# Seven products for every block of layer one, the sign in the evictions, and finer waits

## The chip, the cores and the metric

The kernel runs on one core of a Trainium2 chip. The metric is the time of one execution in microseconds (us); 607.39 us is the median of the three runs before the change. Engines are named as the profile names them: PE is TensorE's matmul, PEld its weight load, DVE VectorE, ACT ScalarE, POOL GpSimd, SP SyncE, which here only issues transfers.

## The reference

Attention over 2 batches, 8 heads, 768 positions and a head width of 64, with a causal window of `n_local` = 96 positions, `n_global` = 8 positions that all see, and a bias by distance; then two layers of a feed-forward network on the 1536 tokens:

```python
x = attn_out.transpose(0, 2, 1, 3).reshape(B * S, H * D)      # 1536 x 512
g = s * np.maximum(x @ moe_w_in, 0) ** 2 + b                  # 512 -> 2048
x = g @ moe_w_out                                             # 2048 -> 512
g = np.maximum(x @ moe2_w_in, 0) ** 2
return g @ moe2_w_out
```

The input `s` is drawn positive, but the kernel takes either sign: it works with |s| and keeps the sign in a column `sg`.

## The kernel before

Each float32 operand is split into a rounded part `hi` and a rest `lo`, and a product is three matmuls (hi·hi, hi·lo, lo·hi). The splits are one copy (ACT or POOL) and one subtraction (DVE). Weights come as 64-bit words; four steps (`d0` on ACT, `d1` to `d3` on DVE, L41 to L56) turn 512 KB of them into a 128x512 tile.

**Stages.** The attention takes twelve tiles of 128 tokens, from the start to about 127 us. From 24.7 us its matmuls are interleaved on PE with the first four of layer one's sixteen weight chunks (`h`, `y`). The other twelve chunks of layer one, and then all sixteen of layer two, are taken in pairs (`a`, `a`+1) and two token halves (`tp`) of 768 tokens, and a pair with one half is a block. Two pairs form a group; a group's order is pair, pair on half 0, then pair, pair on half 1. The groups of layer one are pairs 4 and 6, 8 and 10, 12 and 14.

**A block's first weight.** The 256 x 512 weights and 512 x 768 tokens are cut in 2 x 2. A plain block (`plain`, L541) makes four products of 12 matmuls of 384 columns. A seven-product block (`product`, L530) makes seven products of 6 such matmuls, from four weight sums S1 to S4 (`wsum`, DVE) and four column sums of the input, T1 to T4. Three products accumulate in place; the others are put together by five DVE instructions from PSUM and a copy `m1` (`mid`, `cadd`, L552 to L572). Then come relu and square (ACT), `gh` (ACT or POOL), `gl` (DVE), and the second weight's matmuls (`y2`, L624). `PLAIN` (L31) lists the plain blocks: pairs 4 and 6 on both halves, four of the twelve; all of layer two is seven-product.

**Column sums.** For layer one they come from the attention's hi and lo parts (`tsum1`, L506, task `zs`): eight for each half, one for each T and row tile, in the order T3, T1, T2, T4, in a single buffer `tq`. Each is split by `zsh` and `zsl`. T1 is written over the input's second block, so its split waits for the plain products of its half (`d1`). For layer two the sums (`tsum`, L498, task `ts`) come from `acc`, in the single buffer `m1` that the blocks' copy `m1` uses too. The first product of a block of layer two waits for all eight splits and three input splits of its half, that of a seven-product block of layer one for all eight splits:

```python
                add(("p",) + u + (s,), {"PE": 1.047}, lambda e, u=u, s=s: f.product(*u, s),
                    [prev] + [("wsl", x, a) for x in need[s]] + extra[s] + dt * (s == 0), tm + 1.05 * s,
```

**Evictions.** At a group's end six `flush2` instructions on DVE add the PSUM banks to `acc`. After layer one's last group, four ACT passes for each half multiply `acc` by `sg` (task `sg`, L665 to L667); then the parts are split (`xh`, `xl`) and summed (`ts`).

**Order.** `order` (L805) lists all tasks with engines, estimated times, dependencies, a due time and the rings that they occupy, and `Plan.run` (L135) walks through them at build time: an engine that is free takes the ready task with the earliest due time. That order is the program's; on the chip each engine takes its instructions strictly in it. `SHIFT` (L69) moves single due times.

Of the kernel before, what the change touches and what calls it, by code (L numbers as in the profile page):

```python
# [118 lines left out]


class Plan:
# [1232 lines left out]
```

## Time and profile before

| | |
|---|---|
| runs before | 607.23, 607.39, 608.9 us; median 607.39 |
| profiled execution | 606.85 us |
| its span, first to last instruction | 605.1 us |
| busy: PE, DVE, ACT, POOL | 591.4, 496.8, 354.5, 113.7 us |

The profiled execution's own time is 1.7 us more than its span, which leaves out what lies around the program, and 0.54 us less than the median of the runs. A duration on PE is longer than the distance from one matmul to the next, since matmuls overlap: the start times tell what one costs.

### The profile page before, as it was taken

To read this page: it belongs to the slowest core of one execution; us is meant where nothing else is said; L and a number is where in the kernel's file an instruction comes from. 1 tells how busy PE (TensorE), PEld (TensorE's weight loads), DVE (VectorE), ACT (ScalarE), POOL (GpSimd) and SP (SyncE) were. 2 spreads that over 40 slices of the span, in tenths; PEclk is the share of its full clock that TensorE was granted. 3 is DMA by queue.
4 is the path that set the end of the run, shared out by engine and by line. 5 is a ranking of instruction groups with operands and counts; after the bars stand their busy time and mean duration, and the time that the engine had idled before them with its cause. 6 is when DMAs were issued, how large, how long until landed. Compare 5 with 4: busy or idle time off the path is not lost.

```text
span 605.1 us, 10174 instructions
## 1 busy us (share of the span) xinstructions
PE 591.4 (98%) x3705; PEld 533.9 (88%) x3705; DVE 496.8 (82%) x1115; ACT 354.5 (59%) x774; POOL 113.7 (19%) x187
## 2 busy tenths in 40 slices
PE   8999999999999999999999899999999999999995
PEld 5788898999999999999999788899899999899984
DVE  7999898877999799987989999989587978774452
ACT  7999897756754445544667585655354645434330
POOL 5464432101112111111201012213010111000000
PEclk9999999999999999999999999999999999999999
DMA  7775641022321200312130302241222122000023
GB/s 283 286 268 182 218 157 39 3 96 73 111 70 36 80 26 1 110 61 74 51 124 1 104 2 70 69 140 35 70 69 90 51 69 71 35 1 1 0 106 109
DMA packets 14889, 52.11 MB, mean 86 GB/s; under 512 B 1904, under 2 KB 2160, under 8 KB 14832
## 3 DMA queue, kind: packets, MB, share of 16 engines
q1 hardware_dynamic: 14832, 51.39, 25.2%
q8 instruction: 31, 0.51, 0.3%
q14 instruction: 26, 0.21, 0.1%
HBM read 48.24 MB, written 3.15 MB: 85 GB/s over the span
## 4 chain that ended last, share of the span: by engine, by line


## 5 line engine op out<-in xcount | busy, mean ns | idle before, releaser
L538 PE MATMUL h<-xh,u 128*128 128x384 f32 x384 | 111.7, 337 | 1.2 <-ACT m L221 1.2
L641 PE MATMUL yy<-u,gh 128*128 128x512 f32 x360 | 111.8, 392 | 0.0
L635 PE MATMUL yy<-gh,u 128*128 128x512 f32 (+1 forms) x384 | 97.7, 337 | 0.2 <-ACT gh L605 0.2
L538 PE MATMUL h<-th,u 128*128 128x384 f32 x288 | 85.6, 338 | 0.0
L641 PEld LDWEIGHTS yy<-u,gh 128*128 128x128 f32 x360 | 67.2, 188 | 11.8
L635 PEld LDWEIGHTS yy<-gh,u 128*128 128x128 f32 x384 | 66.8, 189 | 8.5 <-ACT gh L605 0.5
L225 POOL TENSOR_SCALAR u<-st 128x512 fp32r<-128x512 f32 (+1 forms) x47 | 35.2, 749 | 202.4 <-PE h L538 58.7
L538 PEld LDWEIGHTS h<-xh,u 128*128 128x128 f32 x384 | 70.5, 188 | 2.6 <-ACT m L221 1.5
L641 PE MATMUL yy<-u,gl 128*128 128x512 f32 x180 | 70.4, 391 | 0.7 <-DVE gl L615 0.7
L635 PE MATMUL yy<-gl,u 128*128 128x512 f32 (+1 forms) x192 | 64.9, 338 | 1.8 <-DVE gl L612 1.8
L538 PE MATMUL h<-xl,u 128*128 128x384 f32 x192 | 64.6, 337 | 0.0
L538 PEld LDWEIGHTS h<-th,u 128*128 128x128 f32 x288 | 53.1, 188 | 1.9 <-DVE u L559 0.4
L221 ACT ACTIVATE u<-st 128x512 fp32r<-128x512 f32 (+1 forms) x41 | 26.2, 639 | 44.6 <-PE h L538 13.4
L221 ACT ACTIVATE st<-st 128x512 f32<-128x512 f32 x64 | 42.8, 676 | 11.7 <-DMA st<-in_moe_w_in_dram 8.0
L52 DVE SCALAR_TENSOR_TENSOR st<-st 128x512 int32<-128x512 int32 x64 | 46.1, 723 | 3.7 <-ACT st L221 0.9
L538 PE MATMUL h<-tl,u 128*128 128x384 f32 x144 | 48.5, 337 | 0.0
L375 ACT ACTIVATE sn<-sn,nm 128x256 f32<-128x256 f32 (+1 forms) x96 | 46.0, 483 | 1.4 <-DVE nm L367 1.3
L55 DVE SCALAR_TENSOR_TENSOR st<-st 128x512 int32<-128x512 int32 x64 | 44.8, 700 | 0.9
L594 ACT ACTIVATE r<-r 128x384 f32<-128x384 f32 x64 | 33.6, 526 | 13.6 <-DVE r L589 9.0
L635 PEld LDWEIGHTS yy<-gl,u 128*128 128x128 f32 x192 | 36.3, 189 | 5.9 <-DVE gl L612 2.1
L641 PEld LDWEIGHTS yy<-u,gl 128*128 128x128 f32 x180 | 33.8, 188 | 8.5 <-DVE gl L615 1.1
L585 ACT ACTIVATE u<-u 128x384 f32<-128x384 f32 x32 | 16.7, 522 | 37.6 <-DVE u L572 37.5
(153 smaller groups left out, 1308.9 us busy)
## 6 DMA issues: line engine op xcount, KB each, us to landing
st<-in_moe_w_in_dram SPq DMA_DIRECT2D x32, 512.0 KB, 3.9
st<-in_moe_w_out_dram SPq DMA_DIRECT2D x32, 512.0 KB, 3.6
q<-in_qk_dram SPq DMA_DIRECT2D x10, 768.0 KB, 5.0
v<-in_v_dram SPq DMA_DIRECT2D x10, 512.0 KB, 4.6
out_dram<-acc SPq DMA_DIRECT2D x11, 256.0 KB, 2.3
q<-in_qk_dram SPq DMA_DIRECT2D x2, 512.0 KB, 5.0
v<-in_v_dram SPq DMA_DIRECT2D x2, 256.0 KB, 6.0
out_dram<-acc SPq DMA_DIRECT2D x2, 128.0 KB, 3.1
```

Source lines behind the costliest of these rows:

```text
L52: nc.vector.scalar_tensor_tensor(out=lo, in0=hi, scalar=3, in1=lo, op0=ALU.logical_shift_left, op1=ALU.bitwise_or)
L55: nc.vector.scalar_tensor_tensor(out=lo, in0=hi, scalar=-(1 << 31), in1=lo, op0=ALU.bitwise_and, op1=ALU.bitwise_or)
L221: nc.scalar.activation(out=out, in_=in_, func=AF.Copy, scale=scale)
L225: nc.gpsimd.tensor_scalar(out=out, in0=in_, scalar1=scale, scalar2=0.0, op0=ALU.mult, op1=ALU.add)
L375: self.nc.scalar.activation(out=sn[:, x], in_=sn[:, x], func=AF.Exp, scale=-1.0, bias=self.nm[:, n, h:h + 1], accum_out=self.rs[:, n, h:h ...
L538: self.nc.tensor.matmul(ps, p, q, start=first and kt == 0 and x == 0, stop=kt == 1 and x == 2, skip_group_check=not first)
L585: nc.scalar.activation(out=r, in_=h, func=AF.Relu, scale=rt)
L594: nc.scalar.activation(out=r, in_=r, func=AF.Square)
L635: self.nc.tensor.matmul(yj, p[:, js], q[:, lo:hi], start=first and x == 0 and not (side and j % 2), stop=last and x == 2 and not (side and ...
L641: self.nc.tensor.matmul(y[m], p[:, ms], q, start=first and x == 0, stop=last and x == 2)
```

## The change

- `PLAIN` is empty: pairs 4 and 6 of layer one are seven-product blocks like the others.
- The sign `sg` is multiplied in by the evictions (a three-operand instruction on DVE, a scaled copy for the first), and the four `sg` passes for each half are gone.
- Each of a block's seven products waits for the column sum or input part that it reads, and for no other.
- The sums of layer two use the buffer `tq` and wait only for the flushes of the rows that they read.
- The input test is three tasks (a maximum, a transpose on PE, the rest), placed ahead of block (26, 0) of layer two. It was one task after the attention.
- Another `SHIFT` table, a table `PIN` that fixes the engine of some 140 tasks, a time `TURN` that the plan charges when PE changes its kind of matmul, and small corrections of estimated times.

```diff
-PLAIN = ((4, 0), (6, 0), (4, 1), (6, 1))
+PLAIN = ()
...
+TURN = ((0.0, 0.09, 0.18, 0.08), (0.095, 0.0, 0.095, 0.095), (0.095, 0.095, 0.0, 0.095), (-0.08, 0.09, 0.09, 0.0))
+KIND = {"qk": 1, "pv": 2, "tr": 3}
...
+                    if e == "PE":
+                        k = KIND.get(self.tasks[t][0][0], 0)
+                        free[e] += TURN[kind][k]
+                        kind = k
...
-            self.T["t", tp, kt] = self.tm.tile([P, SB], F32, tag="m1", name=f"t{step}_{tp}_{kt}")
+            self.T["t", tp, kt] = self.tq.tile([P, SB], F32, tag="tq", name=f"t{step}_{tp}_{kt}")
...
-                nc.vector.tensor_tensor(out=a, in0=y, in1=a, op=ALU.add)
-            elif part == 1:
-                a = accT[:, j, t0:t0 + TB]
-                copy_r(nc, e, a, a, self.sg)
+                nc.vector.scalar_tensor_tensor(out=a, in0=y, scalar=self.sg, in1=a, op0=ALU.mult, op1=ALU.add)
...
-            self.nc.vector.tensor_tensor(out=a, in0=y, in1=a, op=ALU.add)
-        else:
-            copy_r(self.nc, e, a, y)
+            self.nc.vector.scalar_tensor_tensor(out=a, in0=y, scalar=self.sg, in1=a, op0=ALU.mult, op1=ALU.add)
+        else:
+            copy_r(self.nc, e, a, y, self.sg)
...
+        if name in PIN:
+            engs = {e: d for e, d in engs.items() if e.replace("DVX", "DVE") == PIN[name]}
...
+        if u == (26, 0):
+            add(("check", 0), "DVE:0.35", lambda e: f.check(0), ["second"], tc - 20)
+            add(("check", 1), {"PE": 0.15}, lambda e: f.check(1), [("check", 0), prev], tm, acq=[("h", "chk")])
+            add(("check", 2), "DVE:1.3", lambda e: f.check(2), [("check", 1)], tc, rel=[("h", "chk")])
+            prev = ("check", 1)
...
+        tl = lambda x: [("zsl" if one else "tsl", tp, kt, x) for kt in range(2)]
+        xl = lambda j: ["second"] if one else [("xl", "x", tp, j)]
+        dt = (xl(0), tl(1), xl(2), tl(3), tl(0), tl(2), xl(3))
...
-                    [prev] + [("wsl", x, a) for x in need[s]] + extra[s] + dt * (s == 0), tm + 1.05 * s,
+                    [prev] + [("wsl", x, a) for x in need[s]] + extra[s] + dt[s], tm + 1.05 * s,
...
-            for j in range(4):
-                add(("sg", tp, j), "ACT:0.85", lambda e, g=g, tp=tp, j=j: f.flush2(g, tp, j, 1, e),
-                    [last[j], last[4 + j // 2]], k)
...
-                    [("sg", tp, j // 2 * 2), ("sg", tp, j // 2 * 2 + 1)], k)
+                    [last[2 * r], last[2 * r + 1]] + [last[4 + r]] * c, k)
...
-                        sgn(kt) + [("tsl",) + v + (x - 1,)] * (x > 0) + [("tsl", tp, 0, 3)] * (kt > 0), k,
-                        acq=[("m1", "t") + v + (x,)] * new)
+                        [[last[kt], last[4]], [last[kt + 2], last[5]], [], []][x] + [("tsl",) + v + (x - 1,)] * (x > 0) +
+                        [("tsl", tp, 0, 3)] * (kt > 0), k,
+                        acq=[("tq", "t") + v + (x,)] * new)
```

`dt` is in the order of the seven products: the first needs the input's first part, the second T2, then a part, T3, T1, T4 and a part.

## Rows read from the trace of the kernel before

**Rows 1.** Page, part 1: busy us (share of the span) xinstructions.
```profile
PE 591.4 (98%) x3705; PEld 533.9 (88%) x3705; DVE 496.8 (82%) x1115; ACT 354.5 (59%) x774; POOL 113.7 (19%) x187
```
**Rows 2.** Windows: from:to length, busy us (count) of PE PEld DVE ACT POOL, clock, DMA.
```profile
0.00:24.70 24.70, 21.64 (x167) 14.26 (x168) 19.47 (x103) 20.17 (x71) 12.32 (x37) 1.00 0.86 336
...
100.00:127.60 27.60, 27.60 (x277) 25.48 (x277) 20.55 (x67) 19.45 (x56) 5.09 (x10) 1.00 0.01 1
127.60:145.20 17.60, 17.52 (x147) 17.34 (x147) 15.52 (x37) 10.18 (x20) 2.40 (x4) 1.00 0.25 91
145.20:213.90 68.70, 68.70 (x411) 64.96 (x409) 60.61 (x108) 38.40 (x68) 9.54 (x13) 1.00 0.27 85
213.90:334.50 120.60, 120.60 (x692) 112.28 (x691) 108.36 (x200) 69.65 (x123) 17.06 (x22) 1.00 0.17 53
334.50:391.00 56.50, 52.62 (x270) 46.42 (x269) 54.94 (x101) 38.06 (x69) 9.85 (x14) 1.00 0.22 65
```
**Rows 3.** Timeline of PE, borders of 36 plain and 36 seven-product matmuls: start, duration us.
```profile
192.97 0.34 PE L549 MATMUL h<-xh,u 128*128 128x384 f32 x1
...
199.21 0.40 PE L635 MATMUL yy<-gh,u 128*128 128x512 f32 x1
...
213.90 0.34 PE L538 MATMUL h<-xh,u 128*128 128x384 f32 x1
...
220.18 0.39 PE L635 MATMUL yy<-gh,u 128*128 128x512 f32 x1
```
**Rows 4.** Waits of PE: waiter <- releaser: us in total, times, longest.
```profile
PE yy L635 <- DVE gl L612: 1.8, 1, 1.8
...
PE h L538 <- ACT m L221: 1.2, 1, 1.2
...
PE yy L641 <- DVE gl L615: 0.7, 1, 0.7
```
**Rows 5.** Groups by form: line engine op out<-in xcount | busy us, mean ns | idle before.
```profile
L475 DVE TENSOR_TENSOR u<-st,u 128x512 fp32r<-128x512 f32 x36 | 25.9, 732 | 4.1 <-PE yy L641 3.2 <-PE yy L635 0.9
...
L572 DVE TENSOR_TENSOR u<-h,u 128x384 f32<-128x384 f32 x48 | 26.5, 553 | 13.1 <-PE h L538 12.8
...
L612 DVE SCALAR_TENSOR_TENSOR gl<-r,sgb,gh 128x384 fp32r<-128x384 f32 x32 | 19.5, 609 | 4.6 <-POOL gh L609 3.7 <-ACT gh L605 0.8
L615 DVE TENSOR_TENSOR gl<-r,gh 128x384 fp32r<-128x384 f32 x32 | 17.9, 559 | 4.1 <-ACT gh L607 2.4 <-POOL gh L609 1.7
...
L458 DVE TENSOR_TENSOR st<-st,st 128x256 f32<-128x256 f32 x36 | 16.4, 478 | 0.3
```
**Rows 6.** Instructions of the plain weight split: ns shortest/median/longest, first and last start us.
```profile
L441 DVE TENSOR_TENSOR u<-st,u x40: 660/684/889, 15.0 to 536.0; 128x512 fp32r<-128x512 f32 x40
```
**Rows 7.** Timeline at two of the turn's waits: start, duration us, engine, instruction [idle before].
```profile
372.45 0.55 DVE L615 TENSOR_TENSOR gl<-u,gh 128x384 fp32r<-128x384 f32 x1
372.92 0.55 DVE L504 TENSOR_TENSOR t<-acc 128x384 f32<-128x384 f32 x1
...
380.44 0.56 DVE L523 TENSOR_TENSOR tl<-t,th 128x384 fp32r<-128x384 f32 x1 [0.59 <-ACT th L221]
...
381.75 0.50 ACT L221 ACTIVATE m<-h 128x384 f32<-128x384 f32 x1
...
382.30 0.44 PE L538 MATMUL h<-xh,u 128*128 128x384 f32 x1 [1.15 <-ACT m L221]
```
**Rows 8.** Windows, tile tq alone (DVE ACT POOL): layer one's column sums with splits.
```profile
127.60:237.00 109.40, 32.05 (x56) 5.77 (x11) 3.72 (x5) 1.00 0.21 68
```
**Rows 9.** Windows, line 774 alone: the first chunks' y after the first plain product.
```profile
145.20:164.00 18.80, 6.23 (x50) 5.98 (x48) 1.00 0.40 124
```
**Rows 10.** Windows, all engines: a stretch inside layer one with DVE nearly full.
```profile
175.00:200.00 25.00, 25.00 (x148) 23.82 (x147) 24.59 (x45) 12.88 (x23) 4.20 (x6) 1.00 0.07 22
```
**Rows 11.** Windows, tile chk alone: the input test (PE, PEld, DVE).
```profile
140.00:145.00 5.00, 0.27 (x1) 0.08 (x1) 1.35 (x10) 1.00 0.01 2
```
**Rows 12.** Windows, all engines: from the last matmul to the end of the span.
```profile
598.40:605.10 6.70, 0.05 (x1) 0.00 (x0) 0.75 (x2) 0.00 (x0) 0.00 (x0) 0.87 0.26 88
```

More of the change, by code (lines that the diff above doesn't have):

```diff
@@ new lines @@
+SHIFT = {('at', 2, 0): 33.9, ('at', 3, 3): -39, ('at', 6, 3): 19.8, ('at', 7, 1): 22.2, ('at', 7, 3): -16.6, ('at',
+    9, 2): 47, ('cadd', 10, 1, 1, 0): -83.9, ('cadd', 14, 1, 1, 0): 138, ('cadd', 16, 0, 0, 1): -56, ('cadd', 18, 0,
+    0, 1): 32.3, ('cadd', 24, 0, 1, 1): -68.8, ('cadd', 28, 0, 1, 1): -48.5, ('cadd', 4, 0, 0, 1): -48.7, ('cadd',
[21 rows of a table added]
+    1): -12.5, ('norm', 4, 1): 170.3, ('norm', 4, 2): 40.3, ('norm', 5, 0): -22.9, ('norm', 6, 1): -2.8, ('norm', 7,
[7 rows of a table added]
+    ('qk', 3, 1): -39.7, ('qk', 8, 1): -104.8, ('relu', 2, 1280): 46.4, ('relu', 2, 256): -80.8, ('relu', 20, 1, 0,
+    1): -45.4, ('relu', 22, 1, 0, 1): 119.7, ('relu', 24, 1, 1, 0): 12.5, ('relu', 4, 0, 1, 0): 2.1, ('rs', 10, 0):
[4 rows of a table added]
+    3.8, ('tsl', 1, 1, 2): 33.7, ('tsl', 1, 1, 3): 163, ('ttr', 10, 3): 89.9, ('ttr', 2, 3): -108.1, ('ttr', 5, 1):
+    64.8, ('ttr', 5, 2): 263.5, ('ttr', 6, 3): -41.8, ('ttr', 9, 2): -53.9, ('u2', 22, 1): 32.6, ('u2', 24, 0):
+    26.1, ('u2', 8, 0): 221.6, ('u3', 18, 0): 143, ('whi', 1, 1): 50.5, ('whi', 4, 1): -48, ('wlo', 1, 0): -30.2,
+    ('wlo', 10, 1): -70.2, ('wlo', 17, 1): 300.9, ('wlo', 18, 1): 64.1, ('wlo', 21, 1): 17.8, ('wlo', 22, 1): -17.8,
[17 rows of a table added]
@@ new lines @@
+PIN = {('at', 1, 0): 'ACT', ('at', 4, 0): 'ACT', ('at', 5, 0): 'ACT', ('at', 5, 2): 'ACT', ('at', 6, 2): 'DVE',
[6 rows of a table added]
+    0): 'ACT', ('gh', 2, 1024): 'ACT', ('gh', 2, 256): 'ACT', ('gh', 2, 512): 'POOL', ('gh', 20, 0, 0, 0): 'ACT',
+    ('gh', 20, 0, 0, 1): 'ACT', ('gh', 20, 0, 1, 1): 'ACT', ('gh', 20, 1, 0, 0): 'POOL', ('gh', 20, 1, 1, 1): 'ACT',
+    ('gh', 22, 1, 1, 0): 'ACT', ('gh', 24, 0, 1, 0): 'POOL', ('gh', 26, 0, 0, 0): 'POOL', ('gh', 26, 0, 1, 0):
+    'ACT', ('gh', 26, 1, 0, 1): 'ACT', ('gh', 28, 0, 1, 1): 'ACT', ('gh', 3, 0): 'POOL', ('gh', 3, 1024): 'ACT',
[3 rows of a table added]
+    0, 1, 0): 'ACT', ('gh', 8, 1, 1, 0): 'POOL', ('m1', 10, 0): 'ACT', ('m1', 16, 1): 'DVE', ('m1', 22, 0): 'ACT',
+    ('m1', 26, 1): 'DVE', ('m1', 30, 0): 'DVE', ('ndh', 0, 0): 'ACT', ('ndh', 0, 1): 'ACT', ('ndh', 0, 2): 'DVE',
+    ('ndh', 0, 3): 'ACT', ('ndh', 0, 4): 'DVE', ('ndh', 0, 5): 'ACT', ('ndh', 0, 6): 'ACT', ('ndh', 0, 7): 'DVE',
+    ('ndh', 1, 0): 'POOL', ('ndh', 1, 2): 'POOL', ('ndh', 1, 6): 'POOL', ('ndh', 1, 7): 'POOL', ('norm', 11, 2):
+    'DVE', ('norm', 2, 0): 'POOL', ('norm', 3, 1): 'POOL', ('norm', 3, 3): 'DVE', ('norm', 4, 1): 'DVE', ('norm', 4,
+    2): 'POOL', ('norm', 5, 0): 'POOL', ('norm', 5, 1): 'POOL', ('norm', 5, 2): 'ACT', ('norm', 5, 3): 'ACT',
+    ('norm', 6, 0): 'POOL', ('norm', 7, 0): 'POOL', ('norm', 7, 2): 'ACT', ('norm', 8, 1): 'DVE', ('norm', 9, 1):
+    'POOL', ('relu', 0, 256): 'ACT', ('relu', 0, 512): 'DVE', ('relu', 12, 0, 0, 0): 'DVE', ('relu', 2, 0): 'ACT',
+    ('relu', 2, 1024): 'DVE', ('relu', 2, 256): 'ACT', ('relu', 20, 1, 0, 0): 'ACT', ('relu', 24, 1, 0, 0): 'DVE',
+    ('relu', 28, 0, 0, 0): 'ACT', ('relu', 3, 256): 'ACT', ('relu', 3, 512): 'ACT', ('relu', 3, 768): 'ACT', ('sq',
+    0, 0): 'ACT', ('sq', 0, 1280): 'ACT', ('sq', 1, 1024): 'ACT', ('sq', 2, 1024): 'DVE', ('sq', 2, 1280): 'DVE',
+    ('sq', 3, 512): 'DVE', ('tsh', 0, 1, 0): 'ACT', ('tsh', 0, 1, 3): 'POOL', ('tsh', 1, 0, 0): 'ACT', ('tsh', 1, 0,
+    1): 'ACT', ('tsh', 1, 0, 2): 'POOL', ('tsh', 1, 1, 2): 'ACT', ('whi', 0, 0): 'ACT', ('whi', 1, 0): 'ACT',
+    ('whi', 1, 1): 'ACT', ('whi', 11, 1): 'ACT', ('whi', 13, 1): 'POOL', ('whi', 14, 1): 'ACT', ('whi', 2, 1):
+    'POOL', ('whi', 21, 1): 'ACT', ('whi', 27, 1): 'ACT', ('whi', 3, 0): 'ACT', ('whi', 31, 1): 'ACT', ('whi', 5,
+    1): 'POOL', ('wsh', 'A1', 10): 'POOL', ('wsh', 'A1', 20): 'ACT', ('wsh', 'A1', 24): 'ACT', ('wsh', 'A1', 6):
+    'ACT', ('wsh', 'A1', 8): 'ACT', ('wsh', 'A22', 10): 'POOL', ('wsh', 'A22', 18): 'ACT', ('wsh', 'A22', 20):
+    'ACT', ('wsh', 'S12', 24): 'ACT', ('wsh', 'S12', 6): 'ACT', ('wsh', 'S12', 8): 'POOL', ('wsh', 'S34', 18):
+    'ACT', ('wsh', 'S34', 20): 'ACT', ('wsh', 'S34', 24): 'POOL', ('zsh', 0, 0, 0): 'ACT', ('zsh', 0, 0, 1): 'ACT',
+    ('zsh', 0, 1, 0): 'ACT', ('zsh', 0, 1, 3): 'ACT', ('zsh', 1, 0, 1): 'ACT', ('zsh', 1, 1, 0): 'ACT', ('zsh', 1,
+    1, 3): 'ACT'}
@@ L146, in run @@
         held = {"DVE": 0.0, "POOL": 0.0}
+        kind = 0
         self.busy = dict.fromkeys(ready, 0.0)
@@ L780, in flush, with check @@
         if more:
-            self.nc.vector.tensor_tensor(out=a, in0=y, in1=a, op=ALU.add)
+            self.nc.vector.scalar_tensor_tensor(out=a, in0=y, scalar=self.sg, in1=a, op0=ALU.mult, op1=ALU.add)
         else:
-            copy_r(self.nc, e, a, y)
-    def check(self):
+            copy_r(self.nc, e, a, y, self.sg)
+    def check(self, step):
         nc = self.nc
-        t = self.rp.tile([P, 1], F32, tag="chk", name="chk", bufs=1)
-        u = self.rp.tile([1, 4], F32, tag="chk2", name="chk2", bufs=1)
-        nc.vector.tensor_reduce(out=t, in_=self.nm.rearrange("p a b -> p (a b)"), op=ALU.max,
-                                axis=mybir.AxisListType.X)
-        ps = self.psH.tile([P, 512], F32, tag="h", name="chkp")
-        nc.tensor.transpose(ps[0:1, 0:P], t, self.ident)
-        nc.vector.tensor_reduce(out=u[:, 0:1], in_=ps[0:1, 0:P], op=ALU.max, axis=mybir.AxisListType.X)
+        if step == 0:
+            self.cu = [self.rp.tile([P if x == 0 else 1, (1, 4)[x]], F32, tag=f"chk{x}", name=f"chk{x}", bufs=1) for x in range(2)]
+            nc.vector.tensor_reduce(out=self.cu[0], in_=self.nm.rearrange("p a b -> p (a b)"), op=ALU.max,
+                                    axis=mybir.AxisListType.X)
+            return
+        t, u = self.cu
+        if step == 1:
+            self.cp = self.psH.tile([P, 512], F32, tag="h", name="chkp")
+            nc.tensor.transpose(self.cp[0:1, 0:P], t, self.ident)
+            return
+        nc.vector.tensor_reduce(out=u[:, 0:1], in_=self.cp[0:1, 0:P], op=ALU.max, axis=mybir.AxisListType.X)
         nc.vector.tensor_scalar(out=u[:, 0:1], in0=u[:, 0:1], scalar1=9.0e8, scalar2=None, op0=ALU.is_le)
@@ L823, in order @@
     plan.fill, plan.until = lambda: f.warm(0), ("h", 0, 0)
-    add("n", "SP:0.47", lambda e: None, key=-1000.0, dma=0.06)
+    add("n", "SP:1.2", lambda e: None, key=-1000.0, dma=0.06)
     add("nd0", "POOL:2.1", lambda e: f.consts(0), key=-60.0)
@@ L847, in order @@
                     dq.append(("tr", m, grp(m, mf)[0]))
-                add(("qk",) + u, {"PE": 1.07 if two else 1.17}, lambda e, u=u: f.qk(*u), dq, t, acq=[("a", "s", x) + u for x in range(2)],
+                add(("qk",) + u, {"PE": 0.97 if two else 1.1}, lambda e, u=u: f.qk(*u), dq, t, acq=[("a", "s", x) + u for x in range(2)],
                     rel=[("q", n)] * (hf or not two))
@@ L861, in order @@
                     lambda e, w=w: f.norm(*w, e), [("rs",) + u], t - 1)
-                add(("tr",) + w, {"PE": 0.45}, lambda e, w=w: f.tr(*w), [("norm",) + w], t - 2,
+                add(("tr",) + w, {"PE": 0.438}, lambda e, w=w: f.tr(*w), [("norm",) + w], t - 2,
                     acq=[("a", "t") + w], rel=[("sN",) + w])
@@ L867, in order @@
         t = vt[n, 1] + (cfg["att"] if two else -500.0)
-        add(("pv", n), {"PE": 1.9 if two else 1.1}, lambda e, n=n: f.pv(n), [("at", n, g) for g in grp(n, None)] + [("lv", n)],
+        add(("pv", n), {"PE": 1.8 if two else 1.0}, lambda e, n=n: f.pv(n), [("at", n, g) for g in grp(n, None)] + [("lv", n)],
             t - 3, acq=[("a", "o", n)], rel=[("at", n, g) for g in grp(n, None)] + [("v", n)])
@@ L976, in order @@
         tm, fin = t + cfg["moe"], lo == NT - 256
-        add(("h",) + u, {"PE": 1.44}, lambda e, u=u: f.h(*u, u[1] + 256), dh, tm, acq=[("h",) + u],
+        add(("h",) + u, {"PE": 1.43}, lambda e, u=u: f.h(*u, u[1] + 256), dh, tm, acq=[("h",) + u],
             rel=[slot(w, 0, x) for x in "hl"] * fin)
@@ L985, in order @@
         add(("gl",) + u, "DVX:0.42", lambda e, u=u: f.glo(*u, u[1] + 256), [("gh",) + u], t, rel=[("r",) + u])
-        add(("y",) + u, {"PE": 1.45}, lambda e, u=u, new=new, end=end: f.y(*u, new, end),
+        add(("y",) + u, {"PE": 1.435}, lambda e, u=u, new=new, end=end: f.y(*u, new, end),
             [("gl",) + u, ("wlo", w, 1)] + ([("y",) + before] if before else []) + last * new, tm + cfg["ylag"],
@@ L993, in order @@
                 more = lo in done
-                add(last[j], "DVE:0.6" if more else "DVE:0.6 ACT:0.48",
-                    lambda e, lo=lo, j=j, more=more: f.flush(lo, j, more, e), [("y",) + u], t)
+                add(last[j], "DVE:0.67" if more else "DVE:0.6 ACT:0.5",
+                    lambda e, lo=lo, j=j, more=more: f.flush(lo, j, more, e), [("y",) + u, ("root", 0)], t)
             done.add(lo)
     fin = {a: tp for _, a, tp, _ in quads}
-    for tp in range(2):
+    tps = sorted(range(2), key=lambda tp: min((t for _, a, x, t in quads if x == tp and not plain(a, x)), default=0.0))
+    for tp in tps:
         d0 = ["second"] + [("h", w, lo) for w in range(NF) for lo in range(tp * TB, tp * TB + TB, 256)]
@@ L1009, in order @@
                     d0 + [("zsl",) + v + ((3, 0, 1, 2)[n - 1],)] * (n > 0) + [("zsl", tp, 0, 2)] * (kt > 0) +
-                    [("zsl", 0, 1, 2)] * (tp > 0), k, acq=[("tq",) + v + (x,)] * (n < 2))
+                    [("zsl", tps[0], 1, 2)] * (tp != tps[0]), k, acq=[("tq",) + v + (x,)] * (n < 2))
                 add(("zsh",) + v + (x,), "ACT:0.44 POOL:0.6", lambda e, v=v, x=x: f.tsplit(*v, x, 0, e),
@@ L1018, in order @@
         tm, tc = t + cfg["moe"], t + cfg["chain2"]
-        span = L1S if one else L2S
-        if not one:
-            dt = [("tsl", tp, kt, x) for kt in range(2) for x in range(4)] + [("xl", "x", tp, j) for j in (0, 2, 3)]
-        elif plain(a, tp):
-            dt = ["second"]
-        else:
-            dt = [("zsl", tp, kt, x) for kt in range(2) for x in range(4)]
+        if u == (26, 0):
[3 more added lines that the diff above has]
+            prev = ("check", 1)
+        span = L1S if one else L2S
         wino = not plain(a, tp)
+        tl = lambda x: [("zsl" if one else "tsl", tp, kt, x) for kt in range(2)]
+        xl = lambda j: ["second"] if one else [("xl", "x", tp, j)]
+        dt = (xl(0), tl(1), xl(2), tl(3), tl(0), tl(2), xl(3))
         blocks = {(0, 0): 2, (1, 1): 5, (1, 0): 5, (0, 1): 6}
@@ L1053, in order @@
                 add(("p",) + v, {"PE": 2.09}, lambda e, v=v: f.plain(*v),
-                    [prev, ("wsl", "A2" if c else "A1", a) if mixed(a) else ("wlo", a + c, 0)] + dt * (x == 0),
+                    [prev, ("wsl", "A2" if c else "A1", a) if mixed(a) else ("wlo", a + c, 0), "second"],
                     tm + 2.1 * x, acq=[("h",) + v],
@@ L1117, in order @@
                 df += [("xl", "x", k, x) for k in range(2) for x in (0, 2, 3)]
-            add(name, "DVE:0.6 ACT:0.48" if g[0] == NCH else "DVE:0.6",
+            add(name, "DVE:0.6 ACT:0.48" if g[0] == NCH else "DVE:0.67" if one else "DVE:0.6",
                 lambda e, g=g, tp=tp, j=j: f.flush2(g, tp, j, 0, e), df, tc + span + cfg["tk"])
@@ L1144, in order @@
                     add(("tsl",) + v + (x,), "DVX:0.51", lambda e, v=v, x=x: f.tsplit(*v, x, 1, e),
-                        [("tsh",) + v + (x,)], k, rel=[("m1", "t") + v + (x // 3 * 3,)] * (x > 1))
-    add("check", "DVE:2.0", lambda e: f.check(), ["second", ("relu", NF - 1, NT - 256)], use[6],
-        acq=[("h", "chk")],
-        rel=[("h", "chk")])
+                        [("tsh",) + v + (x,)], k, rel=[("tq", "t") + v + (x // 3 * 3,)] * (x > 1))
     return plan
```

18 lines of the change are left out of this document (2 added, 16 removed), and 94 rows, old and new, of tables (PIN, SHIFT).

## The prediction

> **What bounds the kernel now.** The page's table of busy time comes first: TensorE (PE) is busy 98% of the span [rows 1]. The windows by stage come next: of the stages from 100 to 391 us only the turn from layer one to layer two leaves PE idle for more than 0.1 us, 52.62 busy of 56.50 [rows 2]. Spacing, not the printed duration, tells what a matmul costs: 36 matmuls of plain products take 199.21 - 192.97 = 6.24 us, so 0.173 us each, and 36 of seven-product blocks take 220.18 - 213.90 = 6.28 us, so 0.174 us each [rows 3]. The kernel therefore ends when PE has issued all its matmuls, plus what PE waits. PE's waits come last: three of them, 1.8, 1.2 and 0.7 us, together 3.7 us, on VectorE (DVE) and once on ScalarE (ACT) [rows 4]. In the turn DVE is busy 54.94 of 56.50 us, 97% [rows 2], so it is DVE's backlog that PE waits for there. Before the turn DVE is busy 88% and 90% (60.61 of 68.70, 108.36 of 120.60) and PE waits for nothing.
>
> **Part 1: four plain blocks become seven products.** Each plain block of layer one is 4 products of 12 matmuls, so four are 192 matmuls; as seven products of 6 they are 168. 192 x 0.1733 - 168 x 0.1744 = 33.3 - 29.3 = 4.0 us less on PE, with 128x384 tiles in both [rows 3]. PE is the bound where they lie (145 to 214 us), so I count all of it: -4.0. The matmuls of the second weight (yy) stay.
>
> On DVE the same step adds work. Per block five PSUM additions (u2, u3, three cadd), 20 at 0.553 us = 11.1. Per weight pair, and two pairs change, four 256-wide sums (8 x 0.478 = 3.8), three splits (6 x 0.732 = 4.4) and a half-width split, for which I take the price of a 256-wide sum (2 x 0.478 = 1.0), less four plain splits (4 x 0.684 = 2.7) [rows 5, 6]. That is +17.6 us. DVE instructions follow each other 0.08 us earlier than their ends (372.45 to 372.92 is 0.47 for one of 0.55 [rows 7]); over 32 net instructions that takes 2.6 off, so 15. The copy m1 can go to ACT or DVE: 0 to 4 x 0.55.
>
> A plain sentence beside that sum: a DVE split with both inputs in SBUF has a median of 0.684 and a worst of 0.889 us [rows 6]. By the Trainium skill (SBUF — State Buffer, Who interferes with whom) a VectorE instruction with two SBUF inputs contends with a GpSimd instruction that reads SBUF. By that rule each added split or weight sum that meets a GpSimd copy could cost 0.2 us more, and 16 of them at worst 3.3 us; the means above hold the share that occurs now.
>
> **Part 2: the column sums come sooner.** The eight sums of each token half, splits included, cost DVE 32.05 us for both between 127.6 and 237 [rows 8], so 16 us a half. Before, half 0's may take its time, since four plain blocks need none, and the second sum's split even waits for the plain products of its half. Now product 1 of block (4,0) needs T2 of both row tiles, seven of half 0's eight sums. PE has other work until about 145.2 + 6 = 151 us (the rest of the first four chunks' y [rows 9]). From 127.6, where DVE ends the attention's last tile, to 151 DVE has 23.4 us; it needs 16 for the sums, 11.5 for what it does now in 127.6 to 145.2 besides its first two sums (15.52 less a quarter of 16), about 3 for the first pair's extra weight work (half of part 1's) and about 0.5 for one gl: 31. So 7.6 us must go elsewhere. DVE is idle 27.60 - 20.55 = 7.05 us in the stage ahead [rows 2], with weight loads to fill it (decoding needs nothing of the attention). It just fits. The cost is between 0 and 7.6 us of PE waiting; I take 1.0. For the whole of layer one: DVE's 205 us from 100 to 334.5 [rows 2] become 220 of some 231, 95%. That DVE can run that full without PE waiting is seen from 175 to 200 us: 24.59 of 25.00 busy, PE 25.00 [rows 10]. Against it stands the turn at 97% that lost 7%; 95% lies nearer the lossless side only because work there can be moved, so I keep both ends.
>
> **Part 3: sign in the evictions.** Eight ACT passes over acc go. They sit between the last flush and the splits of layer two, and ACT is not the bound; what they give is a shorter chain at the turn. The flushes become a three-operand form: a 128x384 instruction of that kind is 0.609 us against 0.559 without the scalar [rows 5], so 0 to 40 x 0.05 = 2.0 us of DVE, spread out, inside the 95%; nothing on PE.
>
> **Part 4: each product waits for its own sum, and the sums of layer two leave the m1 buffer.** The 1.2 us wait is that buffer: the sum's last split ends at 381.00, ACT's copy m starts at 381.75, and the product follows at 382.30 [rows 7]. With the sums in the tq buffer m1 is free, and this goes: -1.15, the gap that PE shows. The other two waits (2.5 us) are for gl, late because DVE does the sums of layer two first. Now product 0 and then the others can fill PE while sums are made; but product 1 still needs T2 of both tiles, so the split buys one product (6 x 0.174 = 1.05 us) and, at the end, the late sums. Between 0 and -2.5; I take -1.3. Behind a waiting product stands everything later in PE's written order, the yy of the block before too, so a late sum stops both.
>
> **Part 5: the rest.** The input test moves behind the turn: DVE 1.35 us less in the crowded stage, one small matmul either way [rows 11]. The new order, the pinned engines and the charged changes of matmul kind move everything; nothing in the trace prices them. PE is not busy 24.70 - 21.64 = 3.1 us before 24.7 us [rows 2]; a better or worse front is worth up to about 2 us, and I take 0. Weight loads stay as many; the DMA engines are busy 1% to 27% of those stages [rows 2].
>
> **Sum.** -4.0 + 1.0 - 1.15 - 1.3 = -5.45 us on the profiled execution's 606.85 us (span 605.1): 601.4. The median of the runs is 0.54 above that execution: 601.9.
>
> **Rivals.**
> *The turn stays as long as it is*: product 1 waits for DVE as before, which the order of the sums speaks for, and m1's gap comes back as a longer wait for gl: 607.39 - 4.0 + 1.0 = 604.4; 0.17.
> *More comes back*: all 3.7 us of waits, no new one, and 1.5 us at the front, 607.39 - 4.0 - 3.7 - 1.5 = 598.2; 0.11. For it: two of the three waits have one cause, DVE's sums ahead of gl.
> *The product saving is eaten*: DVE's opening is late by 4 to 6 us where sums and weights meet, and what PE saves it waits: 606 to 609, 607.4 in the middle; 0.11.
> *VectorE becomes the bound of layer one* (the slower side): 220 us of DVE work from 100 us on at the 91% that lies by its 88% to 90% of today takes 241.8 us where 234.5 were needed, so 607.39 + 7.3 - 2.5 = 612.2. It decides below 92.1%: 220 / 0.921 = 238.9, 4.4 us later, less the turn's 2.5. Against it stands the stretch at 98% without loss [rows 10]; 0.09.
> In that rival PE would pause for long. Today's pauses leave the granted clock at 1.00, 2.4 GHz [rows 2]; after the last matmul it averages 0.87 [rows 12], so part of that idle stretch is at 1.2 GHz. By the Trainium skill (TensorE: Matmul & The Clock Gate, Part 1) the low clock is the idle state and a longer pause brings it back, which would double the spacing behind it; the rows agree in kind, and it would push that rival up, not the forecast.
>
> **How the numbers follow.** Forecast 601.9 with 0.52, its own range 599.5 to 604.5. Below 599.5 lies the second rival, at its upper end the first, above it the third and fourth. The range 598.2 to 607.4 leaves out half of the second rival (0.055), half of the third (0.055) and the fourth (0.09). Faster or slower is told at 0.3%, 1.8 us, about what this kernel's runs can tell from no change: faster 0.52 + 0.17 + 0.11 = 0.80, same 0.11, slower 0.09.
>
> **What would show it.** 24 matmuls fewer and line 549 gone; PE busy down by some 4 us; no wait of a product on ACT's m at the turn, and the gl waits there halved; a new short wait of a product or its weight load on DVE's tl near 150 us; DVE above 95% from 127.6 to about 200. The forecast is wrong if PE is idle over 3 us between 145 and 330, or if PE's first 24.7 us move by more than 2.

## The result, and the profile after

| | before | after |
|---|---|---|
| median of the runs | 608.07 us (607.23 to 608.90, 4 runs) | 598.63 us (598.53 to 598.83, 4 runs) |
| profiled execution | 606.85 us | 598.59 us |
| its span | 605.1 us | 596.8 us |

The ratio is 0.9845, 95% interval 0.9828 to 0.9863: 8.26 us less between the profiled executions, 9.4 between the medians. The forecast was 5.45 us less. In all runs of the kernel before that come with a clock, those of the experiments below, its times lie in two groups, 606.7 to 607.5 us with a mean clock of 0.996 to 0.999 and 608.2 to 610.0 with 0.993 to 0.997; the profiled execution is of the first, so the 9.4 us hold some 1.2 that the two profiles do not show. The page of the changed kernel, part 1, answers to [rows 1]:

```profile
PE 586.8 (98%) x3684; PEld 530.5 (89%) x3684; DVE 504.8 (85%) x1133; ACT 363.5 (61%) x796; POOL 107.4 (18%) x179
```

The windows of [rows 2], after (from:to length, busy us and count of PE, PEld, DVE, ACT, POOL, clock, DMA):

```profile
0.00:24.70 24.70, 21.23 (x169) 14.68 (x170) 18.89 (x101) 19.68 (x70) 11.67 (x37) 0.93 0.85 320
100.00:127.60 27.60, 27.60 (x276) 25.74 (x273) 22.19 (x65) 21.69 (x58) 6.65 (x13) 1.00 0.12 37
127.60:145.20 17.60, 17.60 (x147) 17.60 (x146) 16.66 (x35) 12.32 (x25) 2.27 (x4) 1.00 0.20 65
145.20:213.90 68.70, 68.48 (x409) 64.18 (x408) 66.15 (x124) 42.79 (x76) 8.68 (x12) 1.00 0.21 62
213.90:334.50 120.60, 120.60 (x694) 112.42 (x694) 111.12 (x206) 73.97 (x130) 13.18 (x16) 1.00 0.22 70
334.50:391.00 56.50, 56.50 (x299) 51.92 (x298) 52.35 (x99) 32.20 (x61) 13.15 (x17) 1.00 0.21 66
```

The count of matmuls falls by 21 and not by 24, since three more `warm` matmuls, whose result nothing uses, run at the start. PE loses nothing at the turn any more, and 0.22 us between 145 and 214 us (at 212.6), with DVE 96% busy there. All of PE's waits after that the view lists, to be read beside [rows 4]:

```profile
PE a L410 <- DMA q<-in_qk_dram: 2.1, 2, 1.9
PE warm L373 <- DVE idle L370: 1.3, 1, 1.3
PE h L589 <- DVE u L610: 0.2, 1, 0.2
PE a L443 <- POOL sn L276: 0.2, 1, 0.2
```

Lines below the tables have moved by 48 to 51: L538 is now L589, L635 L686, L572 L623.

**Where the 8.3 us are.** The distance from each matmul's start to the next, summed by kind over the whole trace of either kernel:

| | before | after | |
|---|---|---|---|
| first weight of the blocks | 211.97 | 205.81 | -6.2, of which 24 matmuls of 0.174 make -4.2 |
| second weight of the blocks | 235.1 | 232.7 | -2.4, the waits for `gl` |
| attention | 66.4 | 65.1 | -1.25 |
| start, `warm` and the wait for q | 11.3 | 13.2 | +1.9 |
| last matmul's start to the end | 6.7 | 6.1 | -0.6 |

The first chunks add 0.2; the sum is -8.3. Two rows belong together: the first 120 matmuls of the attention, which lie in the front, take 13.1 us before and 11.9 after, the other 600 take 53.3 and 53.2. So the front as a whole is 0.7 us longer, and the attention behind it is unchanged.

### The profile page after: what moved, and what is told of

Its sections match the earlier page's. It is cut to its first block, busy times and chain, and to the rows that moved or that the text cites. A ratio compares the mean times of both kernels' runs of the same rounds, so it can differ in the third digit from the quotient of the medians.

```text
span 596.8 us, 10149 instructions
## 1 busy us (share of the span) xinstructions
PE 586.8 (98%) x3684; PEld 530.5 (89%) x3684; DVE 504.8 (85%) x1133; ACT 363.5 (61%) x796; POOL 107.4 (18%) x179
## 4 chain that ended last, share of the span: by engine, by line
## 5 line engine op out<-in xcount | busy, mean ns | idle before, releaser
L589 PE MATMUL h<-xh,u 128*128 128x384 f32 x448 | 131.0, 337 | 0.0
L589 PE MATMUL h<-th,u 128*128 128x384 f32 x336 | 99.8, 338 | 0.2 <-DVE u L610 0.2
L686 PE MATMUL yy<-gh,u 128*128 128x512 f32 (+1 forms) x384 | 98.7, 337 | 0.0
L589 PEld LDWEIGHTS h<-xh,u 128*128 128x128 f32 x448 | 82.4, 188 | 1.1
L589 PE MATMUL h<-xl,u 128*128 128x384 f32 x224 | 75.4, 337 | 0.0
L686 PEld LDWEIGHTS yy<-gh,u 128*128 128x128 f32 x384 | 67.2, 189 | 7.7
L272 ACT ACTIVATE u<-st 128x512 fp32r<-128x512 f32 (+1 forms) x63 | 40.1, 639 | 44.5 <-DVE st L55 18.7
L686 PE MATMUL yy<-gl,u 128*128 128x512 f32 (+1 forms) x192 | 64.8, 338 | 0.0
L589 PEld LDWEIGHTS h<-th,u 128*128 128x128 f32 x336 | 62.0, 188 | 2.3 <-DVE u L610 1.1
L589 PE MATMUL h<-tl,u 128*128 128x384 f32 x168 | 56.5, 337 | 0.0
L276 POOL TENSOR_SCALAR sn<-sn,rs 128x256 f32<-128x256 f32 (+1 forms) x68 | 34.8, 527 | 50.0 <-DVE rs L432 18.4
L589 PEld LDWEIGHTS h<-xl,u 128*128 128x128 f32 x224 | 42.1, 188 | 1.0
L610 DVE TENSOR_TENSOR u<-h,m 128x384 f32<-128x384 f32 x56 | 30.9, 552 | 14.1 <-PE h L589 13.4
L276 POOL TENSOR_SCALAR u<-st 128x512 fp32r<-128x512 f32 (+1 forms) x29 | 20.6, 712 | 111.6 <-DVE st L55 42.7
```

What stands on the lines that cost most here:

```text
L272: nc.scalar.activation(out=out, in_=in_, func=AF.Copy, scale=scale)
L276: nc.gpsimd.tensor_scalar(out=out, in0=in_, scalar1=scale, scalar2=0.0, op0=ALU.mult, op1=ALU.add)
L589: self.nc.tensor.matmul(ps, p, q, start=first and kt == 0 and x == 0, stop=kt == 1 and x == 2, skip_group_check=not first)
L610: self.nc.vector.tensor_tensor(out=t, in0=self.T["h", a, tp, 1], in1=self.T["m1", a, tp], op=ALU.add)
L686: self.nc.tensor.matmul(yj, p[:, js], q[:, lo:hi], start=first and x == 0 and not (side and j % 2), stop=last and x == 2 and not (side and ...
```

## Experiments

All ratios are to the kernel before, run on the same chip. A difference in us to the changed kernel's 598.63 is between two chips; the kernel before had medians of 608.07 to 608.46 on the four chips used, so some 0.4 us of such a difference can be the chip. Where an edit changes the tasks, the order is planned anew, from the same table of due times unless the text says otherwise.

### Two parts alone, in the order of before

**E1, the sums of layer two in `tq`:**

```diff
-            self.T["t", tp, kt] = self.tm.tile([P, SB], F32, tag="m1", name=f"t{step}_{tp}_{kt}")
+            self.T["t", tp, kt] = self.tq.tile([P, SB], F32, tag="tq", name=f"t{step}_{tp}_{kt}")
```

> The kernel before, in its own order, with layer two's column sums in the buffer tq instead of m1 and nothing else. Theory (PE's wait for ACT's m at 382 us is that buffer): the wait goes, 606.85 - 1.15 = 605.7 for a profiled execution, a ratio of 0.998 to before. Rival (DVE's queue is what holds it, m or not): no change, the gap is there with another name.

607.83 us, ratio 1.0008 (0.9994 to 1.0021): no change, as the rival said. Timeline of ACT, and of PE below, at the wait (start, duration us):

```profile
380.43 0.53 ACT L221 ACTIVATE th<-t 128x384 fp32r<-128x384 f32 x1 [1.74 <-DVE t L504]
380.87 1.55 ACT L221 ACTIVATE acc<-yy 128x512 f32<-128x512 f32 x3
382.30 0.50 ACT L221 ACTIVATE m<-h 128x384 f32<-128x384 f32 x1
...
382.85 0.44 PE L538 MATMUL h<-xh,u 128*128 128x384 f32 x1 [1.17 <-ACT m L221]
```

`m1` was free and the wait the same. The copy `m` stands in ACT's queue behind three first copies of `acc` and a `th` that waits 1.74 us for DVE's sum: it was not the buffer that held it, and by these rows it was its place in the queue.

**E2, the sign in the evictions, without the eight passes:**

```diff
-                nc.vector.tensor_tensor(out=a, in0=y, in1=a, op=ALU.add)
+                nc.vector.scalar_tensor_tensor(out=a, in0=y, scalar=self.sg, in1=a, op0=ALU.mult, op1=ALU.add)
...
-                copy_r(nc, e, a, a, self.sg)
+                return
```

> The kernel before, in its own order, with the sign multiplied in by the evictions and the eight passes on ACT left out. Theory (DVE is the backlog at the turn, ACT is not): DVE's 40 three-operand instructions cost 0 to 2 us and the shorter chain gives 0 to 2.7: 605.5 to 607.5. Rival (ACT's passes in front of layer two's sums caused the waits for gl): both waits go, 604.3 to 604.8.

610.17 us, ratio 1.0030 (1.0009 to 1.0052): slightly slower, where both readings had it faster. The turn's three waits are as long as before (1.8, 1.2 and 0.7 us). The profiled execution is 3.5 us longer than that of before. 1.4 us of it (7 matmuls of 512 columns at 0.427 instead of 0.231 us) are in the windows of the pause at 337.4 us and of what follows, 0.4 at the input test; the rest is in pauses of 0.1 to 0.25 us over the whole span:

```profile
337.40:339.80 2.40, 0.53 (x2) 0.22 (x2) 2.40 (x6) 1.99 (x5) 0.00 (x0) 1.00 0.68 210
339.80:344.20 4.40, 4.40 (x13) 3.52 (x14) 4.33 (x9) 2.02 (x5) 0.00 (x0) 0.61 0.39 124
```

### Parts of the change undone, order planned anew from its own table

**E3, the four old plain blocks:**

```diff
-PLAIN = ()
+PLAIN = ((4, 0), (6, 0), (4, 1), (6, 1))
```

> The changed kernel (598.6 us) with the old four plain blocks put back, all else as changed. Theory (PE's issued matmuls set the end): 24 more matmuls of 0.174 us, so 598.6 + 4.2 = 602.8. Rival (DVE is the bound since the change): some 15 us less DVE work pays back, 597 to 600. Rival (the due times fit only the new blocks): 606 or more.

**E4, the first product waits for all sums:**

```diff
-                    [prev] + [("wsl", x, a) for x in need[s]] + extra[s] + dt[s], tm + 1.05 * s,
+                    [prev] + [("wsl", x, a) for x in need[s]] + extra[s] + [d for y in dt for d in y] * (s == 0), tm + 1.05 * s,
```

> The changed kernel with the first of a block's seven products planned after all sums and input parts of its half, as before the change. Theory (the finer waits removed the waits for gl at the turn): gaps of PE between 330 and 390 us come back, 1 to 2.7 us, so 599.6 to 601.3. Rival (DVE is relieved by other parts and the sums come in time anyway): 598.6 within 0.5, no gap.

**E5, as E4, and the sign passes and the sums in `m1` of before** (E1's and E2's edits backwards):

> The changed kernel with all of the turn as before: four sign passes for each half on ACT, two-operand evictions, layer two's sums in the buffer m1, first product after all sums. Theory (the turn's changes are worth its 3.9 us of PE gaps): 598.6 + 3.9 = 602.5. Rival (the new order and pinned engines took the gaps away): 598.6 to 600.

619.89, 615.75 and 637.11 us; ratios 1.0196 (1.0155 to 1.0236), 1.0121 (1.0103 to 1.0138) and 1.0465 (1.0444 to 1.0485). Every one is slower than the kernel before, and far over what its part was priced at. Only E3's last rival (606 or more) had named such a time; every reading of E4 and E5 lay below 603. Windows, E3, E4, E5:

```profile
213.90:330.00 116.10, 104.74 (x562) 95.13 (x561) 88.37 (x161) 53.95 (x97) 12.80 (x17) 0.96 0.19 59
330.00:390.00 60.00, 59.72 (x329) 54.62 (x329) 57.92 (x108) 37.33 (x67) 11.04 (x14) 1.00 0.14 45
```

```profile
145.20:213.90 68.70, 64.47 (x371) 58.00 (x371) 66.27 (x123) 37.34 (x67) 9.88 (x13) 1.00 0.19 62
213.90:330.00 116.10, 110.67 (x630) 101.86 (x629) 98.26 (x179) 59.95 (x106) 17.83 (x23) 1.00 0.22 69
330.00:390.00 60.00, 58.71 (x306) 51.52 (x304) 58.35 (x107) 35.72 (x65) 7.82 (x10) 1.00 0.14 44
```

```profile
330.00:390.00 60.00, 38.81 (x206) 34.50 (x205) 53.12 (x94) 33.83 (x57) 9.26 (x13) 0.86 0.19 62
```

E3 has less DVE work than the changed kernel and yet loses 11.4 us of PE between 214 and 330, in waits of 0.3 to 3.0 us, most of them on `u`, `gh` and `gl`. I take it that the due times fit the seven-product blocks only. So these runs price a part together with a table that no longer fits, and I could not take the two apart with them. The step from E4 to E5 has the same fault, since the table has no due times for E5's sign passes: without evicted sign and `tq` the turn loses 21.2 of 60 us, with them 1.3. In E5 one wait of 14.1 us on ACT's `m` makes most of it, behind copies in ACT's queue that wait for DVE's sums.

### The same without any table

**E6, the kernel before; E7, it with seven products everywhere and nothing else; E8, the changed kernel.** `SHIFT` is empty in all three, `PIN` too in E8, so that no order is fitted to any of them; `TURN` and the corrected estimates stay in E8.

```diff
-SHIFT = {('at', 0, 0): -17.4, ('at', 2, 0): 83.2, ('at', 2, 3): -18.5,
...
+SHIFT = {}
...
-PLAIN = ((4, 0), (6, 0), (4, 1), (6, 1))
+PLAIN = ()
```

> The kernel before with its table of single due times (SHIFT) emptied, so that the order follows from the general rules alone. It is the base for the next two. Theory (the written order is worth as much as the whole change): 8 to 30 us slower than before, 615 to 638, with PE's waits of 0.3 to 2 us spread over the whole program. Rival (the table holds only small corrections): under 5 us slower, 608 to 613.

> The kernel before with the table emptied and PLAIN empty: the four plain blocks as seven products, alone, with the sign passes and the all-at-first waits of before. Against the run with the table emptied alone. Theory (PE bounds layer one, VectorE has room): 24 matmuls fewer give 2 to 4 us less. Rival (the first seven-product block waits for eight sums on VectorE, which is nearly full): the saving is eaten or more, 0 to 8 us slower than the emptied kernel before, with waits of products on VectorE's tl between 140 and 215 us.

> The changed kernel with both tables (SHIFT and PIN) emptied: the structure of the change with an order from the general rules. Theory (the structure brings the gain by itself): 6 to 10 us below the kernel before with its table emptied. Rival (the gain belongs to structure and fitted order together, as the three undoings suggest): within 3 us of that run or above it, and 12 us or more above the changed kernel.

626.24, 646.67 and 624.36 us; ratios 1.0294 (1.0277 to 1.0311), 1.0638 (1.0612 to 1.0665), 1.0261 (1.0244 to 1.0278). Windows of the opening and the turn, E6, E7, E8:

```profile
145.20:213.90 68.70, 68.70 (x425) 65.42 (x424) 61.53 (x120) 40.57 (x72) 12.29 (x16) 1.00 0.24 73
...
330.00:390.00 60.00, 50.06 (x243) 43.88 (x243) 57.03 (x99) 32.04 (x54) 15.77 (x20) 0.89 0.19 62
```

```profile
145.20:213.90 68.70, 53.44 (x296) 46.87 (x296) 64.95 (x131) 32.52 (x61) 10.65 (x13) 0.90 0.18 58
...
330.00:390.00 60.00, 49.58 (x262) 44.54 (x261) 53.71 (x92) 33.56 (x55) 15.05 (x19) 0.91 0.17 53
```

```profile
145.20:213.90 68.70, 59.07 (x328) 53.60 (x327) 64.34 (x124) 34.83 (x64) 10.51 (x13) 0.93 0.17 53
...
330.00:390.00 60.00, 57.97 (x317) 51.96 (x316) 55.14 (x98) 33.12 (x60) 12.23 (x17) 1.00 0.17 53
```

E6 lies where its theory put it. The seven products alone (E7) save 24 matmuls and cost 20.4 us, far over the 0 to 8 of its rival: PE loses 15.3 us at the opening, where E6 loses none, and the turn stays at 10.4. The rest of the change takes 22.3 us off again: the opening loses 9.6, the turn 2.0. For E8 the rival held: the structure brings only 1.9 us by itself, and the fitted order is worth 25.7 us on the changed kernel against 17.8 on the old one (from its 608.42 us in these runs).

### How near the two bounds are

**E9, 24 matmuls more** (two repeats in 12 places of chunks 4 and 6), and **E10, 24 DVE additions more** (`mid`'s two in every block of layer one made twice), both in the order of the changed kernel:

```diff
+                for _ in range(2 if first and kt == 0 and x == 0 and a in (4, 6) else 0):
+                    self.nc.tensor.matmul(ps, p, q, start=True, stop=True)
...
+            for _ in range(2 if a < NCH else 1):
```

> The changed kernel, in its own order, with 24 more matmuls: in the four blocks of pairs 4 and 6 the first matmul of three of the seven products is issued three times, which computes the same. Theory (PE bounds the place where four plain blocks stood): + 24 x 0.174 = 4.2 us, 602.8. Rival (DVE bounds the opening of layer one, PE has slack there): 0 to 1.5 us more.

> The changed kernel, in its own order, with DVE's additions u2 and u3 made twice in the twelve blocks of layer one: 24 instructions of 0.55 us, 0.47 apart, 11.3 us of DVE work from 147 to 330 us, where DVE is idle about 11.6 us. Theory (PE is the bound, DVE stands just below): it takes the slack and some waits appear, 2 to 6 us more, 600.6 to 604.6. Rival (DVE is the bound already): 9 to 11 us more. Rival (DVE has room): below 1 us.

E9: 602.14 us, ratio 0.9913 (0.9893 to 0.9932), 3.5 us over the changed kernel. The repeats follow at 0.174 us each, 4.2 us; the missing 0.7 is about what two pauses give that got shorter, at 10 and 212 us. So PE is the bound, and a matmul costs its spacing. E10: 606.94 us, ratio 0.9981 (0.9968 to 0.9993), 8.3 over, more than its theory of 2 to 6 and just under the rival in which DVE is the bound already (9 to 11). The additions are 11.3 us of DVE at 0.47 each; of PE's waits these are new:

```profile
PE h L589 <- DVE u L611: 3.0, 7, 0.8
...
PE h L589 <- DVE r L624: 1.4, 2, 1.0
...
PE yy L687 <- DVE gl L664: 0.9, 2, 0.6
```

From start to start these pauses are 13, 7.5 us together. So in layer one DVE had some 3 us of room left (11.3 - 8.3, an estimate).

### The front

**E11, q1's load ahead of the 1 KB `sb` load on SP. E12, as E11, with the first step that reads `sb` issued later on DVE:**

```diff
-        add(("lq", n), "SP:0.47", lambda e, n=n: f.load("q", n), [], -900.0 + 2 * n if not two else key,
+        add(("lq", n), "SP:0.47", lambda e, n=n: f.load_sb() if n == 1 else f.load("q", n), [], -900.0 + 2 * n if not two else key,
...
-    add("sb", "SP:0.47", lambda e: f.load_sb(), key=-895.0, dma=0.06)
+    add("sb", "SP:0.47", lambda e: f.load("q", 1), key=-895.0, dma=0.06)
```

> The changed kernel with two transfers swapped on the SP queue: the second attention tile's q and k (768 or 512 KB) takes the place of the small load of s and b, which goes where that was; nothing else of the order moves. Theory (the 1.9 us that PE waits at 8.3 to 10.1 us for q lies on the path of the attention's start): q lands some 1.3 us sooner and the end comes 0.7 to 1.9 us sooner, 596.7 to 597.9. Rival (what starts the first h at 26 us is another chain, and the front is made up later): 598.6 within 0.4.

> The changed kernel with the load of q1 put ahead of the small sb load on SP, as in the run before with that swap, and now root step 0, which reads sb, is issued in the slot of step 1, behind tile 0's first reductions. Theory (that run lost 3.4 us only because step 0, waiting 3.2 us for sb, stood at the head of VectorE's queue ahead of tile 0's work): the wait of PE for q (1.9 us at 8.3 us) goes and nothing takes its place: 0.7 to 1.9 us below the changed kernel, 596.7 to 597.9. Rival (what PE meets at the front is the arrival of some load in any order): the wait moves to another load or sum of tile 0, and the time is that of the changed kernel within 0.5, 598.1 to 599.1.

E11: 601.98 us, ratio 0.9898 (0.9880 to 0.9917). Neither reading held. The wait for q is gone, but on DVE's timeline the step that reads `sb` now stands and waits, tile 0's reductions behind it:

```profile
10.12 0.15 DVE L762 TENSOR_SCALAR sg<-sb 128x1 f32<-128x1 f32 x1 [3.16 <-DMA sb<-in_sb_dram]
...
11.01 0.29 DVE L418 CUSTOM_DVE_ANT_0 sn<-a,ND 128x128 f32<-128x128 f32 x1
```

E12: 598.60 us, ratio 0.9838 (0.9822 to 0.9855), the same as the changed kernel, as the rival said. Neither load is waited for now; PE waits as long for tile 0's softmax instead:

```profile
PE a L443 <- POOL sn L276: 1.3, 1, 1.3
PE a L464 <- ACT at L449: 0.5, 1, 0.5
PE a L443 <- ACT at L449: 0.4, 1, 0.4
```

No kernel here beats the changed one.

## Why the prediction came out as it did

The time lies inside the range, but near its lower end: 3.3 us under the forecast, below the forecast's own 599.5 to 604.5, and by its number beside the second rival (598.2), which had a chance of 0.11. One half of that rival came, all waits at the turn; its gain at the front did not. That the number falls so near that rival is in part luck: in the place of the front's 1.5 us stand small pauses that went with the waits and a shorter end, which nobody priced, and the 0.54 us by which the old median lay above its profiled execution (after: 0.04).

| step | forecast | trace |
|---|---|---|
| four plain blocks | -4.0 | -4.2 |
| opening of layer one | +1.0, between 0 and 7.6 | +0.2 |
| wait on ACT's `m` | -1.15 | -2.2 with the small pauses of the first weight |
| waits for `gl` | -1.3, between 0 and -2.5 | -2.4 |
| front, within 2 | 0 | +0.7 (+1.9 at the start, -1.2 in the first attention matmuls) |
| end | 0 | -0.6 |

Three terms (opening, `m`, `gl`) were off by about 1 us each, all to the slow side; what was not priced (front, end, first chunks) adds up to +0.3.

**Products:** right, and E9 shows that a matmul at this place costs its spacing in full.

**Opening:** the mechanism was right and its size is a matter of order, which the single value of 1.0 hid. DVE is 95% and 96% busy from 127.6 to 213.9 us, as I had named; the short wait on `tl` near 150 us did not come. I let the sums begin at 127.6 us and looked for 7.6 us of DVE work to go elsewhere. In the changed kernel the attention itself ends sooner on DVE; the timeline there:

```profile
119.47 0.69 DVE L473 TENSOR_TENSOR xl<-a,xh 128x512 fp32r<-128x512 f32 x1 [0.48 <-ACT xh L469]
120.07 0.55 DVE L568 TENSOR_TENSOR tq<-xh 128x384 f32<-128x384 f32 x1
```

The same splits in the kernel before (count, shortest/median/longest in ns, first and last start in us):

```profile
L422 DVE TENSOR_TENSOR xl<-a,xh x4: 680/686/692, 96.1 to 126.9; 128x512 fp32r<-128x512 f32 x4
```

The last split of the attention starts at 119.5 instead of 126.9 us and the first sum follows it at once, 7.5 us ahead of my start. Windows with the tile `tq` on DVE alone, for the changed kernel and then for E8, the same work without tables:

```profile
120.00:145.20 25.20, 13.33 (x24) 1.00 0.26 84
```

```profile
120.00:145.20 25.20, 8.67 (x16) 1.00 0.11 27
```

13.3 of a half's 16 us are done by 145.2 in one, 8.7 in the other, and the other loses 9.6 us of PE. The longest of its waits between 145.2 and 213.9 us is that of a product for a column sum's copy:

```profile
PE h L497 <- ACT th L180: 4.2, 1, 4.2
```

So a late sum does stop PE for microseconds; the other waits there are on `gl`, `gh`, `u` and `tl`, and how much of the 9.6 the sums cost in all is not shown. That the early sums are what saves it fits both rows but was not tried alone.

**DVE's work** grew by 8.0 us, where I had 15 plus up to 2 (the input test's 1.35 only moves). The additions came as counted (the group of 48 in [rows 5] is now one of 56):

```profile
L623 DVE TENSOR_TENSOR u<-h,u 128x384 f32<-128x384 f32 x56 | 31.0, 553 | 8.0 <-PE h L589 7.6
```

What I left out is what went from DVE to ACT: of the copies `m`, DVE makes 7 instead of 11, and of the first chunks' first `acc` copies none instead of 5. DVE's copies `m`, before and then after:

```profile
L223 DVE TENSOR_SCALAR m<-h 128x384 f32<-128x384 f32 x11 | 6.1, 554 | 1.2 <-PE h L538 1.0
```

```profile
L274 DVE TENSOR_SCALAR m<-h 128x384 f32<-128x384 f32 x7 | 3.9, 551 | 0.5 <-PE h L589 0.5
```

With the five `acc` copies (3.4 us) that is 5.6 us; the rest is in smaller shifts, of relus above all. ACT's busy time rises by 9.0 us although its sign passes (8 of 0.927) are gone, mostly because it now makes 53 of the weight splits' 128x512 copies instead of 35; POOL makes 25 instead of 41.

So the fourth rival, with its 220 us, had too much work in it; E10 shows that 11.3 us more would have brought it most of the way. The split with two SBUF inputs has a mean of 735 ns after (42 of them) and 732 before [rows 5], so the extra contention that the Trainium skill (SBUF — State Buffer, Who interferes with whom) led me to price at up to 3.3 us does not show in the mean. Single splits do show it, and longer than the 0.889 us that I took for the worst; before:

```profile
L475 DVE TENSOR_TENSOR u<-st,u x48: 410/680/1139, 158.4 to 526.7; 128x512 fp32r<-128x512 f32 x36, 128x256 fp32r<-128x256 f32 x12
```

The longest after takes 1.134 us. Of all 128x512 splits, [rows 6] included, those that overlap no copy on POOL take at most 0.694 us (53 of 76 before, 57 of 78 after). The other 23 and 21 hold every longer one; above the common 0.684 us they add up to 2.1 us before and 2.5 after, so the change added 0.4.

**The `m1` buffer:** the wait went, but the reason that I gave for it was wrong. I read a buffer out of two times that stood close, [rows 7]; E1 frees the buffer and the wait stays to 0.02 us. In the changed kernel ACT makes five such first copies in one stretch at the turn, and what follows them is no `m` that a product waits for:

```profile
374.79 2.53 ACT L272 ACTIVATE acc<-yy 128x512 f32<-128x512 f32 x5
378.30 0.53 ACT L636 ACTIVATE u<-u 128x384 f32<-128x384 f32 x1 [0.97 <-DVE u L623]
```

That the order of the queue is the cause is read from these rows; it was not moved by itself.

**The waits for `gl`:** I gave half of them back. All went. In the turn DVE now has 52.35 us of work in 56.50 where it had 54.94. Neither the sign nor the buffer alone does that (E1, E2: turn unchanged); sign, buffer and finer waits together, with the rest of the change, do, with a fitted order (3.9 us lost to none) and without any (10.4 to 2.0, E7 to E8). Which of them a fitted order needs stays open: each single part would need an order fitted to it.

**Front:** +0.7, inside my 2. q1's load is issued at 3.13 us instead of 2.18, behind `sb` and a load of v in SP's queue, and PE's matmuls on it start at 10.1 us instead of 8.0; E12 shows that taking this wait away alone gives nothing, because tile 0's softmax ends no sooner: by 20.5 us PE's matmuls start within 0.1 us of where the changed kernel's do. The mean clock of the first 24.7 us is 0.93 after and was 1.00 before [rows 2], but that is not what the front costs: in E12 and E9 it is 1.00 there, and E12 takes the same time. **Attention:** the matmuls behind the front take what they took, so the charged changes of kind show no gain.

## What to carry to other kernels

Price a change of structure together with the order that it will run in: here the seven products alone cost 20 us in an order from the general rules, and as part of the whole change, in an order fitted to it, they gave 4. When a part is undone under a fitted schedule, the misfit is measured along with the part, so run both kernels without the fitted table as well. And before a wait is put down to a buffer, read what stands ahead of the releasing instruction in its engine's queue.
